# Moving TensorE's branch hint from the last down projection to the first combination

## The chip, the cores and the metric

The kernel runs on one core of a Trainium2 chip. The metric is the device time of one execution in microseconds (us), lower is better; several runs are taken and their median is given. A core has five engines with an instruction stream each: TensorE (PE, with PEld for its weight loads), VectorE (DVE), ScalarE (ACT), GpSimd (POOL) and SyncE (SP). Here SyncE issues all transfers of data.

## The reference

A gated linear attention feeds a soft mixture of experts. Per head (4 batches, 8 heads, 768 steps, 48 channels) a state is decayed by a gate and read by the query:

```
f = 1 / (1 + exp(-f_logit))
for t in range(768):
    state = f[:, :, t, :, None] * state + einsum('bhd,bhe->bhde', k[:, :, t], v[:, :, t])
    y[:, :, t] = einsum('bhd,bhde->bhe', q[:, :, t], state)
```

The outputs, laid side by side as x (3072 tokens, 384 channels), go through the mixture (8 experts, 4 slots each, 1024 hidden):

```
logits = x @ phi                                   # 3072 x 32
d = softmax of logits over the tokens;  slot_input = d.T @ x
slot_out[e] = maximum(slot_input[e] @ w1[e], 0) @ w2[e]
c = softmax of logits over the slots;   return c @ slot_out
```

## The kernel before

All arithmetic is in float32. The attention runs in 24 blocks of 128 tokens, in the chunked form (scores, masks, a state carried from block to block). It needs gates whose running products stay within a bound; the kernel computes beside the result a flag that says whether they do.

The mixture's tail follows the last block. `up` multiplies the 32 slot inputs with w1, `turn` transposes the hidden values, and then come three parts of 128 output channels each. For part p there are four down projections `dn{p}0` to `dn{p}3` (function `down`, matmuls at L822, 16 products of 128x128 in each), a copy (L830), one matmul that sums over the experts (L834), a copy into `s4` (L838), two combinations `cb{p}0` and `cb{p}1` (function `combine`, matmuls at L845), copies of the result into staging buffers (L854, L856, L859) and stores (L863), issued by SyncE.

The order on each engine is written down ahead of time by a planner, the class `Plan`: every operation is added with a cost, its dependences and a due time, `plan.schedule()` picks an order, and a loop over `plan.order` then emits the instructions in it. For TensorE the planner also counts instructions: a product costs `INS` = 4, a page holds `PAGE` = 256 of them, and a page is entered no sooner than `FETCH` = 5.8 us (a constant of the planner's costs) after the one before.

After the last operation each engine loads the flag into a register (`values_load`, L1038) and branches on it (`tc.If`, L1040). If the flag is set, a slow general computation, `general()`, follows. With the inputs here it isn't set, and every engine jumps over that code to a short closing part: at L1040 SyncE waits for the eight stores in flight, at L1095 all engines meet in a barrier.

Code for the general case is long, so the target of the jump lies far behind the branch. A branch hint is an instruction that each engine has ahead of its branch and that names the branch; its kind here is "LikelyTaken". The dictionary `hints` says ahead of which operation it stands: for SyncE, GpSimd, ScalarE and VectorE ahead of `si` (a copy, L757, at about 122 us), for TensorE ahead of `dn23`, the last down projection (it follows `dn22` in a run of 64 matmuls and loads that starts at 148.95 us). `cb00` is the first combination. On TensorE it starts at 142.19 us, behind the expert sum `so0` and one transposition, `ct5` (L704, 141.65 us). From there TensorE's order is `cb00`, `dn12`, `dn13`, `cb01`, `so1`, `dn20`, `dn21`, `cb11`, `dn22`, `dn23`, and after it `cb10`, `so2`, `cb20`, `cb21` and the branch.

Of the kernel before, what the change touches and what calls it, by code (L numbers as in the profile page):

```python
# [278 lines left out]
def gla_soft_moe_kernel(ctx: ExitStack, tc: tile.TileContext, q, k, f, v, fd, qd, kd, vd, phi, w1, w2, out):  # L279
# [13 lines left out]
    def P(shape, name, dt=F32):  # L293
        return pool.tile(shape, dt, tag=name, name=name)
# [60 lines left out]
    wb, wd, si = P([128, 1], "wb"), P([128, NS], "wd"), P([128, 3, NS], "si")  # L355
# [603 lines left out]


    EN = mybir.EngineType
    hints = {"si": [EN.SP, EN.Pool, EN.Activation, EN.DVE], "dn23": [EN.PE]}
    port = None
    for o in plan.order:
        if o["name"] in hints:
# [136 lines left out]
```

## Time and profile before

| | |
|---|---|
| median of 3 runs | 164.95 us (164.65 to 165.14) |
| the profiled execution: time, span | 164.98 us, 163.2 us |
| granted clock of TensorE, mean | 0.987 |
| busy: TensorE, VectorE, ScalarE, GpSimd | 147.3, 120.3, 99.0, 26.2 us |
| bytes moved | 54.01 MB in 17571 packets |
| q1 (data), q8 and q14 (instructions) | 17536, 21 and 14 packets |
| TensorE's hint, branch, next instruction | 149.2, 153.6, 156.2 us |
| end of the span | 163.2 us |

The span runs from the first instruction to the last; the time of an execution also has what lies around it. Times in the views are microseconds from the span's start. Letter q behind an engine's name marks its sequencer, which waits, branches and issues; these are not counted as the engine's busy time. A row of a line's view gives the operation, its count, the shortest, median and longest duration in nanoseconds, and the first and last start. The rows of the hints carry the line L1095, those of the branch L1040.

### The profile page before, as it was taken

To read this page: it belongs to the slowest core of one execution; us is meant where nothing else is said; L and a number is where in the kernel's file an instruction comes from. 1 tells how busy PE (TensorE), PEld (TensorE's weight loads), DVE (VectorE), ACT (ScalarE), POOL (GpSimd) and SP (SyncE) were. 2 spreads that over 40 slices of the span, in tenths; PEclk is the share of its full clock that TensorE was granted. 3 is DMA by queue.
4 is the path that set the end of the run, shared out by engine and by line. 5 is a ranking of instruction groups with operands and counts; after the bars stand their busy time and mean duration, and the time that the engine had idled before them with its cause. 6 is when DMAs were issued, how large, how long until landed. Compare 5 with 4: busy or idle time off the path is not lost.

```text
span 163.2 us, 5865 instructions
## 1 busy us (share of the span) xinstructions
PE 147.3 (90%) x2461; PEld 112.6 (69%) x2461; DVE 120.3 (74%) x234; ACT 99.0 (61%) x186; POOL 26.2 (16%) x43
## 2 busy tenths in 40 slices
PE   2998999999999999999999999999999999999600
PEld 2987777688877797878877887778753248777300
DVE  6789998899999999989999999999371113250410
ACT  4998977796959888783886967743440130033520
POOL 4001111050305020060306322160011000000000
PEclk9999999999999999999999999999999999999995
DMA  4999999999999799999999988618999998046891
GB/s 149 346 404 386 407 419 398 383 374 413 390 377 381 267 381 368 382 329 350 387 407 375 319 315 253 241 24 353 428 426 420 420 418 345 16 180 231 332 375 66
DMA packets 17571, 54.01 MB, mean 331 GB/s; under 512 B 1920, under 2 KB 5120, under 8 KB 14464
## 3 DMA queue, kind: packets, MB, share of 16 engines
q1 hardware_dynamic: 17536, 53.55, 87.0%
q8 instruction: 21, 0.34, 0.8%
q14 instruction: 14, 0.11, 0.2%
HBM read 48.82 MB, written 4.72 MB: 328 GB/s over the span
## 4 chain that ended last, share of the span: by engine, by line
PE 61%; DVE 14%; ACT 8%; DMA 7%; issue 3%; SPq 2%; POOL 1%; ACTq 0%; DVEq 0%; POOLq 0%
PE pr L541 12%; PE pr L581 6%; PE sg L612 6%; PE pr L572 5%; PE pr L788 5%; PE sg L822 5%; DVE as L544 4%; DMA ag<-in_f_dram 4%; PE sg L630 3%; PE sg L532 3%; PE pr L845 3%; DMA aq<-in_q_dram 3%; PE sg L659 2%; PE sg L553 2%; PE pr L822 2%
## 5 line engine op out<-in xcount | busy, mean ns | idle before, releaser
L544 DVE TENSOR_TENSOR as<-pr,tri 128x1024 f32<-128x1024 f32 x24 | 29.1, 1214 | 2.2 <-PE pr L541 1.5
L541 PE MATMUL pr<-aq,ak 48*128 48x128 f32 x384 | 27.9, 285 | 0.4 <-DVE as L544 0.2
L541 PEld LDWEIGHTS pr<-aq,ak 48*128 48x128 f32 x384 | 23.3, 187 | 5.0 <-issue 2.5
L581 PE MATMUL pr<-as,av 128*48 128x128 f32 x384 | 24.1, 274 | 1.2 <-DVE as L544 1.0
L581 PEld LDWEIGHTS pr<-as,av 128*48 128x48 f32 x384 | 20.2, 123 | 2.9 <-DVE as L544 2.1
L612 PE MATMUL sg<-ident,xT 128*128 128x128 f32 x96 | 15.2, 282 | 0.4 <-ACT ag L535 0.2
L527 POOL TENSOR_TENSOR aq<-aq,ac 128x512 f32<-128x512 f32 x9 | 11.4, 1281 | 25.0 <-ACT ac L502 8.7
L584 ACT COPY xT<-pr 128x512 f32<-128x512 f32 x20 | 11.5, 582 | 5.5 <-PE pr L581 5.4
L524 POOL TENSOR_TENSOR ak<-ak,af 128x512 f32<-128x512 f32 x6 | 7.7, 1279 | 35.3 <-ACT af L501 23.4
L572 PE MATMUL pr<-aq,st 48*48 48x128 f32 x320 | 13.1, 278 | 0.2 <-DVE aq L527 0.2
L502 ACT ACTIVATE ac<-ac 128x1024 f32<-128x1024 f32 (+1 forms) x13 | 12.9, 993 | 0.5
L612 PEld LDWEIGHTS sg<-ident,xT 128*128 128x128 f32 x96 | 10.4, 141 | 3.6 <-issue 1.5
L854 ACT COPY hm<-pr 128x768 f32<-128x768 f32 x7 | 5.5, 802 | 10.9 <-PE pr L845 10.9
L532 PE MATMUL sg<-ident,ak 128*128 128x128 f32 x80 | 11.9, 282 | 0.0
L487 DVE TENSOR_TENSOR_SCAN ac<-chain,af 128x256 f32<-128x256 f32 x16 | 10.9, 681 | 1.1 <-issue 1.1
L535 ACT COPY ag<-sg 128x512 f32<-128x512 f32 x17 | 9.4, 586 | 3.7 <-PE sg L532 3.7
L615 ACT COPY xr<-sg 128x384 f32<-128x384 f32 x17 | 8.1, 479 | 4.9 <-PE sg L612 4.8
L488 DVE TENSOR_TENSOR_SCAN ac<-chain,af 128x256 f32<-128x256 f32 x16 | 10.6, 665 | 0.0
L553 PEld LDWEIGHTS sg<-av,ag 128*48 128x48 f32 x320 | 8.6, 124 | 2.7 <-issue 1.2
L527 DVE TENSOR_TENSOR aq<-aq,ac 128x512 f32<-128x512 f32 x15 | 10.2, 685 | 0.3 <-POOL ak L524 0.2
L572 PEld LDWEIGHTS pr<-aq,st 48*48 48x48 f32 x320 | 8.0, 119 | 3.4 <-issue 2.0
L532 PEld LDWEIGHTS sg<-ident,ak 128*128 128x128 f32 x80 | 8.6, 141 | 2.2 <-issue 0.9
(142 smaller groups left out, 243.0 us busy)
## 6 DMA issues: line engine op xcount, KB each, us to landing
hm<-in_w_dram SPq DMA_DIRECT2D x17, 1024.0 KB, 8.0
ak<-in_k_dram SPq DMA_DIRECT2D x24, 256.0 KB, 5.9
aq<-in_q_dram SPq DMA_DIRECT2D x24, 256.0 KB, 5.8
av<-in_v_dram SPq DMA_DIRECT2D x24, 192.0 KB, 5.4
af<-in_f_dram SPq DMA_DIRECT2D x7, 512.0 KB, 5.6
out_dram<-hm SPq DMA_DIRECT2D x8, 384.0 KB, 3.8
ag<-in_f_dram SPq DMA_DIRECT2D x4, 512.0 KB, 5.9
out_dram<-hm SPq DMA_DIRECT2D x2, 768.0 KB, 4.3
```

What stands on the lines that cost most here:

```text
L487: nc.vector.tensor_tensor_scan(cx[:, : 2 * BT], chain, lx[:, : 2 * BT], 0.0, op0=ALU.mult, op1=ALU.add)
L502: add(f"p{n}", {"ACT": t_act(w)}, lambda e: nc.scalar.activation(flat(c_), flat(c_), AF.Exp, scale=-1.0), w=cs, prio=T(n, 1.2))
L527: tt(e)(flat(q_), flat(q_), flat(c_), op=ALU.mult)
L532: nc.tensor.transpose(pk[:, a], k_[:, a], ident)
L541: nc.tensor.matmul(ps[:, r, a], k_[rows[r], col(a)], queries(r, a), start=True, stop=True)
L544: tt(e)(sc_.rearrange("p r (m x) t -> p (r m) (x t)", x=2), bank(("sc", n)).rearrange("p r (m t) -> p (r m) t", m=2), tri.rearrange("p x t ...
L553: nc.tensor.matmul(pk[rows[r], col(a)], kp_[:, col(a), rows[r]], v_[:, 2 * a + r], start=True, stop=True)
L572: nc.tensor.matmul(py[at : at + D, r, a // 2], s0[rows[r], col(a)], queries(r, a), start=a < 2, stop=False, skip_group_check=True)
L581: nc.tensor.matmul(py[at : at + D, r, a // 2], v_[:, 2 * a + r], sc_[:, r, a], start=first and a < 2, stop=a >= 2, skip_group_check=True)
L584: copy(e)(xT[:, n % NXT].rearrange("p (r m) t -> p r (m t)", r=2), bank(("y", n))[:, :, : 2 * BT])
L612: nc.tensor.transpose(px[:, i], xT[:, n % NXT, i], ident)
L822: nc.tensor.matmul(po[32 * qq : 32 * qq + 32, :w], hT[:, j, 4 * kh + kk, 32 * qq : 32 * qq + 32], t[:, qq, kk], start=(j, kh, kk) == (0, 0 ...
```

## The change

TensorE's hint stands ahead of `cb00` instead of `dn23`. The other engines' hints and all operations stay where they are.

```
-    hints = {"si": [EN.SP, EN.Pool, EN.Activation, EN.DVE], "dn23": [EN.PE]}
+    hints = {"si": [EN.SP, EN.Pool, EN.Activation, EN.DVE], "cb00": [EN.PE]}
     port = None
     for o in plan.order:
         if o["name"] in hints:
             tc.mark_branch_hint_location("general", hint="LikelyTaken", engines=hints[o["name"]])
```

More of the change, by code (lines that the diff above doesn't have):

```diff
@@ L961, in gla_soft_moe_kernel @@
     EN = mybir.EngineType
-    hints = {"si": [EN.SP, EN.Pool, EN.Activation, EN.DVE], "dn23": [EN.PE]}
+    hints = {"si": [EN.SP, EN.Pool, EN.Activation, EN.DVE], "cb00": [EN.PE]}
     port = None
```

## The prediction

> **What bounds the kernel now.** I read the page first (busy shares, queues), then the chain of waits over the last 15 us, then the rows of the branch (L1040) and of its hints (recorded under L1095), and last the DMA queues in windows a tenth of a microsecond wide, because the hint can act only through an instruction fetch.
>
> The page: span, TensorE's busy time, the share of the chain, the two instruction queues.
>
> ```profile
> span 163.2 us, 5865 instructions
> PE 147.3 (90%) x2461; PEld 112.6 (69%) x2461; DVE 120.3 (74%) x234; ACT 99.0 (61%) x186; POOL 26.2 (16%) x43
> PE 61%; DVE 14%; ACT 8%; DMA 7%; issue 3%; SPq 2%; POOL 1%; ACTq 0%; DVEq 0%; POOLq 0%
> q8 instruction: 21, 0.34, 0.8%
> q14 instruction: 14, 0.11, 0.2%
> ```
>
> TensorE sets the time up to its last matmul. Queue q8 moved 0.34 MB in 21 packets, 16.2 KB each. TensorE ran 2 x 2461 = 4922 matmuls and weight loads; over 256 (the planner's PAGE) that is 19.2 pages, close to 21 packets. So I read q8 as TensorE's instruction stream, a page to a packet, and q14 as that of the other engines.
>
> The chain of waits over the end (start us, us, what), then the store and what SyncE does after the branch:
>
> ```profile
> 149.02 1.88 PE sg L822 x64
> 150.91 0.87 PE pr L845 x8
> ...
> 152.82 1.24 PE pr L845 x10
> ...
> 155.39 0.70 ACT hm L854
> ```
> ```profile
> L863 SPq DMA_DIRECT2D out_dram<-hm x10: 332/386/721, 144.2 to 156.4; - x10
> DMA to landing us min/median/max: 3.3/3.8/5.5
> ```
> ```profile
> L1040 SPq EVENT_SEMAPHORE  x8: 17/17/17, 161.1 to 161.9; - x8
> L1040 POOLq COMPARE_BRANCH  x1: 65/65/65, 123.4 to 123.4; - x1
> L1040 POOLq EVENT_SEMAPHORE  x1: 17/17/17, 128.7 to 128.7; - x1
> L1040 PEldq COMPARE_BRANCH  x1: 2482/2482/2482, 153.6 to 153.6; - x1
> L1040 ACTq COMPARE_BRANCH  x1: 68/68/68, 155.3 to 155.3; - x1
> L1040 DVEq COMPARE_BRANCH  x1: 84/84/84, 155.5 to 155.5; - x1
> L1040 PEldq EVENT_SEMAPHORE  x1: 51/51/51, 156.2 to 156.2; - x1
> L1040 ACTq EVENT_SEMAPHORE  x1: 17/17/17, 158.3 to 158.3; - x1
> L1040 SPq COMPARE_BRANCH  x1: 70/70/70, 158.9 to 158.9; - x1
> L1040 DVEq EVENT_SEMAPHORE  x1: 21/21/21, 159.3 to 159.3; - x1
> ```
> ```profile
> L1095 PEldq EVENT_SEMAPHORE  x2: 51/51/51, 162.7 to 163.2; - x2
> L1095 POOLq BRANCH_PREFETCH_HINT  x1: 43/43/43, 120.5 to 120.5; - x1
> ...
> L1095 DVEq BRANCH_PREFETCH_HINT  x1: 56/56/56, 122.5 to 122.5; - x1
> L1095 PEldq BRANCH_PREFETCH_HINT  x1: 45/45/45, 149.2 to 149.2; - x1
> ```
>
> The end is set thus: ScalarE's last copy ends at 155.39 + 0.70 = 156.1; SyncE issues the last store at 156.4; at the slowest landing, 5.5 us, it is down at 161.9, when the last of SyncE's eight semaphore waits at L1040 passes. The closing barrier ends at 163.2, and 1.78 us lie outside the span (164.98 - 163.2). TensorE's branch is the odd one: 2.48 us long, where the others record 65 to 84 ns. TensorE goes on at 156.2 and then waits for the closing barrier until 162.7: 6.5 us of slack behind the branch.
>
> **The change part by part.** The hint is one instruction of 45 ns on TensorE's sequencer. No wait, no issued transfer of data and no engine's order changes, and SP's and POOL's queues are not passed; the four other hints stay.
>
> First, the instruction itself. At the old place it is taken out of a stretch in which the matmul array is busy all the time, so nothing is gained there. At the new place it stands ahead of the first combination, where TensorE idles for VectorE's copy anyway:
>
> ```profile
> 141.65 0.27 PE L704 MATMUL sg<-ident,ltok 128*128 128x128 f32 x1
> 142.19 0.93 PE L845 MATMUL pr<-ltok,xT 32*128 32x384 f32 x8 [0.28 <-DVE xT L838]
> ```
> ```profile
> 142.00:146.00 4.00, 3.81 (x81) 2.52 (x82) 1.65 (x4) 0.90 (x2) 0.00 (x0) 1.00 0.25 95
> 146.00:150.00 4.00, 4.00 (x114) 3.13 (x117) 1.16 (x2) 1.61 (x3) 0.00 (x0) 1.00 0.79 302
> ```
> ```profile
> L834 PEldq EVENT_SEMAPHORE  x1: 51/51/51, 141.0 to 141.0; - x1
> ```
>
> The sequencer passes its last semaphore before that place at 141.0 (L834) and is held at the combination until VectorE's copy ends, shortly before 142.19. The 0.045 us lie inside that. Without this cover they cost 0.045 us, 0.03%. Taken: 0.
>
> Second, the fetch. In five answers of the DMA view, for 137.7 to 137.8, 143.3 to 143.4, 149.9 to 150.0, 153.4 to 153.5 and 158.1 to 158.3 us in this order, q8 has one packet each; the last line is 133 to 156 us, where it has these first four and no other:
>
> ```profile
> q8 instruction: 1, 0.02, 63.8%
> q8 instruction: 1, 0.02, 83.2%
> q8 instruction: 1, 0.02, 58.6%
> q8 instruction: 1, 0.02, 75.3%
> q8 instruction: 1, 0.02, 30.0%
> q8 instruction: 4, 0.07, 1.2%
> ```
>
> The share is that of 16 engines' time in the window, so the packets took 0.638 x 1.6 = 1.02, then 1.33, 0.94, 1.20 and (0.300 x 3.2) 0.96 us. The pages at 137.7, 143.3 and 149.9 come 5.6 and 6.6 us apart, at the pace of the stream. The one at 153.4 comes only 3.5 us later, starts before the branch (153.6) and is followed by TensorE's next instruction: it is down at 153.45 + 1.20 = 154.65, and TensorE goes on at 156.2, so 1.5 us pass from landing to use. I take it for the target's page, called by the hint 4.2 us earlier, and the branch's 2.48 us for the wait until it can be used. With the hint at about 141.1, 12.5 us ahead of the branch, the page should be there in time: the branch falls from 2.48 us to some 0.07 (like the others' 65 to 84 ns), and TensorE is through at 153.7. What hides this gain is SyncE's path, to which TensorE's 156.2 is not a party: the barrier waits for SyncE at 161.9. Taken: 0. If that cover were gone, the gain would be the 2.4 us.
>
> Third, the place of the fetch among the transfers. Now it takes 1.20 us on one of 16 DMA engines while the stores run, and the last stores land in up to 5.5 us where the fastest takes 3.3. Out of their way, the last landing can only come earlier, but SyncE itself does not reach its eight waits before 161.1, so the end moves by at most 161.9 - 161.1 = 0.8 us. At the other end, TensorE's next page (158.2 us now) simply moves to another place among the same stores: 0. I take 0, since all eight waits need time of their own after 161.1 and the fetch is one packet among a full queue's.
>
> Fourth, the fetch of the stream itself. At the new place the hint falls close to the page at 143.3. No row shows what two close calls on TensorE's fetch do to each other, so I bound it: 0, if they run side by side or the stream goes first, to a stall of the size of the two rivals below. I take 0: the hint's call stood behind a page of the stream in this trace too (149.9, 153.4), and TensorE was not held by it, with 4.00 of 4.00 us busy up to 150.
>
> Sum: 0 + 0 + 0 + 0 on 164.98 us of the profiled execution, which stands 0.03 us above the median of three runs, 164.95. Forecast: 164.95 us, no measurable change.
>
> [...]
>
> **The rivals.** *The hint does nothing there.* The target is dropped, or is fetched only when the stream reaches the branch's page. For it: GpSimd's hint at 120.5 stood 2.9 us ahead of its branch, VectorE's at 122.5 stood 33 us ahead, and both still waited 5.3 and 3.8 us behind the branch. Against it: TensorE's own fetch came ahead of its branch. At worst TensorE waits as GpSimd did, 5.3 us, and goes on at 153.6 + 5.3 = 158.9, still 3.8 us ahead of the barrier at 162.7. Time: 164.95.
>
> *The hint's page delays the page of the stream (slower).* If TensorE's fetches run one after another, the pair at 149.9 and 153.4 gives the pace, 3.5 us. A hint at 141.1 is served first, at about 143.3, and the stream's page follows at 146.8 rather than 143.3; it lands at about 147.8 and can be used at 149.3. It is needed 256 instructions after the page before: at (114 + 117) / 4.00 = 58 instructions per us in the window from 146 that is 4.4 us, and from the fetch at 143.3, called around 142.2, at 146.6 by the sequencer; its matmuls run up to 1 us later, at 147.6 to 147.9. TensorE would stand for about 149.3 - 147.9 = 1.4 us, and the chain is TensorE from there to 154.1 with hardly a gap. Time: 166.35; 0.5 us or less if the stream's page is called first or nearly so. It decides from the point where the hint is executed before the stream crosses into its next page, which the rows do not settle: 141.0 for the last semaphore before it, 143.3 for the page's packet.
>
> *The hint's page takes the place of the stream's next page (slower).* Then TensorE meets a missing page, whose price the rows of the branch show on other engines: 158.9 to 161.1 on SyncE is 2.2 us, on GpSimd 5.3. Time: 167.2 to 170.2. [...]
>
> *Faster.* The last stores land sooner without the fetch at 153.4 among them; at the 0.8 us bound that is 164.15; I price it at three quarters of the bound, 164.35. For it: landings between 3.3 and 5.5 us. Against it: one packet of 1.2 us on one engine, and SyncE's own 161.1.
>
> **How the numbers follow.** Three runs spread from 164.65 to 165.14; about 0.3%, 0.5 us, is what can be told from no change. Forecast with the page there in time 0.33; hint without effect 0.26; stream delayed 0.22, of which 0.02 within 0.3%; place taken 0.09; faster 0.10. So faster 0.10, same 0.61, slower 0.29. The likeliest time, 164.95, has 164.6 to 165.3 as its own range; the range for 8 in 10 runs from 164.3 (the larger part of the faster case) to 166.7 (the delayed stream and the spread of runs) and leaves out the taken place and part of the faster case.
>
> **What would show it.** Right: TensorE's branch below 0.1 us; its q8 packet for the target between 141 and 148 and none at 153; TensorE's last matmul still starting near 154.0; the last of SyncE's waits still at 161.9. Wrong: TensorE idle between 146 and 150, with "issue" as its releaser and no semaphore behind it (stream delayed or place taken); a branch still of 2.5 us, or a gap of 3 to 5 us behind it (no effect); the last landing before 161.4 (faster).

## The result, and the profile after

The changed kernel is slower. Beside the kernel before, with eight runs of each, its median was 165.85 us (165.26 to 166.22) against 164.96 us, a ratio of 1.0052 with a 95% interval of 1.0033 to 1.0071. Its profiled execution took 166.22 us, of which the span has 164.5.

TensorE's arithmetic is untouched. Three lines of the page after, then the windows by engine, then two pieces of the chain of waits (start us, us, what): from 146 to 150 us TensorE is busy for the same 4.00 us, and the last matmuls and ScalarE's last copy follow as before, 0.29 us later.

```profile
span 164.5 us, 5865 instructions
...
PE 147.7 (90%) x2461; PEld 112.9 (69%) x2461; DVE 120.2 (73%) x234; ACT 99.1 (60%) x186; POOL 26.2 (16%) x43
...
q8 instruction: 20, 0.33, 0.8%
```
```profile
146.00:150.00 4.00, 4.00 (x106) 3.05 (x106) 1.16 (x2) 1.41 (x2) 0.00 (x0) 1.00 0.80 308
```
```profile
153.11 1.24 PE pr L845 x10
...
155.68 0.70 ACT hm L854
```

The rows of the branch and of the hint, from the engines' sequencers (count, shortest, median and longest duration in ns, first and last start):

```profile
L1040 SPq EVENT_SEMAPHORE  x8: 17/17/17, 162.6 to 163.1; - x8
...
L1040 PEldq COMPARE_BRANCH  x1: 388/388/388, 153.9 to 153.9; - x1
L1040 PEldq EVENT_SEMAPHORE  x1: 51/51/51, 154.9 to 154.9; - x1
...
L1040 SPq COMPARE_BRANCH  x1: 70/70/70, 160.0 to 160.0; - x1
```
```profile
L1095 PEldq BRANCH_PREFETCH_HINT  x1: 45/45/45, 141.4 to 141.4; - x1
```

The hint does what it says. It stands at 141.4 us, TensorE's branch falls from 2.48 to 0.39 us, and TensorE is through at 154.9 instead of 156.2. Its stream of instructions does not hold it up, with 4.00 of 4.00 us busy from 146 to 150. But SyncE reaches its branch at 160.0 instead of 158.9 and its eight waits at 162.6 instead of 161.1. The reason stands one step earlier in SyncE's work, in the issues of the stores (L863; the second line is their landing):

```profile
L863 SPq DMA_DIRECT2D out_dram<-hm x10: 332/364/1677, 144.5 to 157.9; - x10
DMA to landing us min/median/max: 2.3/3.7/4.9
```

The longest issue takes 1677 ns where it was 721, and the last starts at 157.9 instead of 156.4. In order of time (start us, us), SyncE in two overlapping windows after, and in two before:

```profile
155.71 2.10 SPq L863 DMA_DIRECT2D out_dram<-hm  x2
...
156.13 2.52 SPq L863 DMA_DIRECT2D out_dram<-hm  x2
```
```profile
155.84 0.41 SPq L863 DMA_DIRECT2D out_dram<-hm  x1
...
156.36 0.72 SPq L863 DMA_DIRECT2D out_dram<-hm  x1
```

The two rows of after say that the issue at 155.71 and the next one end together at 157.81, and that the next one starts at 156.13: it is the one of 1.68 us, against 0.41 us before. Queue q8 in the window 156.05 to 156.15 us of the changed kernel:

```profile
q8 instruction: 1, 0.02, 82.8%
```

A page of TensorE's instructions starts in that tenth of a microsecond and takes 0.828 x 1.6 = 1.32 us. It is the page that TensorE calls once it has jumped: it starts 1.2 us behind TensorE's next instruction (154.9), where it came at 158.2 before, 2.0 us behind (156.2), and where the branch is held it moves along with it (e13, e14 and e1 below). Reading on the trace's own clock, it starts at 156.10, 0.03 us ahead of the issue, and is down at 157.43; the issue ends 0.38 us after that.

About 0.3 us of this execution's 1.3 us more of span have another cause: TensorE's matmuls at L788 stand at 128.80 instead of 128.51 us, 12 us ahead of any difference between the kernels. From execution to execution the start of ScalarE's last copy moves between 154.8 and 155.7 us whatever the hint. So below I also give the stretch from the start of ScalarE's last copy (155.27 before, 155.57 after) to the end of the span: 7.97 us before, 8.92 after.

### The profile page after: what moved, and what is told of

Its sections match the earlier page's. It is cut to its first block, busy times and chain, and to the rows that moved or that the text cites. A ratio compares the mean times of both kernels' runs of the same rounds, so it can differ in the third digit from the quotient of the medians.

```text
span 164.5 us, 5865 instructions
## 1 busy us (share of the span) xinstructions
PE 147.7 (90%) x2461; PEld 112.9 (69%) x2461; DVE 120.2 (73%) x234; ACT 99.1 (60%) x186; POOL 26.2 (16%) x43
## 4 chain that ended last, share of the span: by engine, by line
PE 58%; DVE 12%; DMA 11%; ACT 8%; SPq 3%; issue 2%; ACTq 0%; DVEq 0%
PE pr L541 10%; DMA av<-in_v_dram 6%; PE pr L581 6%; PE sg L612 5%; PE pr L788 5%; PE pr L572 5%; DMA aq<-in_q_dram 5%; PE sg L822 4%; DVE as L544 4%; PE sg L630 3%; SPq L456 3%; PE pr L845 3%; PE sg L659 2%; PE sg L532 2%; PE sg L553 2%; PE pr L822 2%
```

## The experiments

My theory after the comparison: *a page of TensorE's instructions that meets a store issue of SyncE holds that issue until the page is down, and the early hint moves the page after the branch onto the fifth of the last six issues.* The rivals: *the early hint costs by itself*, through its fetch among the stores or in the stream, and *drift*, that is, nothing but the spread between executions.

The table sums up all profiles; the runs are told below it. "Page" is the start of TensorE's pages on q8 from 4 us ahead of ScalarE's last copy on, counted from that copy's start; SyncE's last four issues start at -0.56, 0.14, 0.56 and 1.1 in each of them where none is held. "Held to" gives the start of TensorE's branch. "Issue" is the longest of these four, "stretch" runs from that copy's start to the end of the span; all in us.

| run | hint, TensorE's branch | page | issue | stretch | ratio (95% interval) |
|---|---|---|---|---|---|
| before | last down | -1.83, 2.92 | 0.72 | 7.97 | |
| e6, before again | last down | -1.77, 2.85 | 0.93 | 8.22 | |
| e16, before again | last down | -1.25, 3.50 | 0.72 | 7.99 | |
| after | first combination | 0.53 | 1.68 | 8.92 | 1.0052 (1.0033 to 1.0071) |
| e5, after again | first combination | 0.65 | 1.49 | 8.47 | 1.0016 (0.9996 to 1.0036) |
| e9, after again | first combination | 0.66 | 1.48 | 8.40 | 1.0001 (0.9972 to 1.0030) |
| e15, after again | first combination | 0.68 | 1.69 | 8.46 | 1.0052 (1.0031 to 1.0072) |
| e13 | first combination, held to 155.4 | 2.90 | 0.72 | 7.94 | 0.9988 (0.9973 to 1.0002) |
| e14 | first combination, held to 156.5 | 3.90 | 0.72 | 8.10 | 1.0005 (0.9984 to 1.0027) |
| e1 | first combination, held to 157.2 | 4.62 | 0.71 | 8.41 | 0.9990 (0.9965 to 1.0015) |
| e10, e1 again | first combination, held to 157.8 | 4.73 | 0.72 | 8.14 | 0.9997 (0.9976 to 1.0019) |
| e2 | last down, held to 156.9 | -0.15, 4.88 | 1.02 | 9.19 | 1.0022 (1.0000 to 1.0044) |
| e3 | none | 0.62, 5.16 | 1.49 | 8.82 | 1.0010 (0.9983 to 1.0037) |
| e4 | behind the last down | -3.28, 0.31 | 1.75 | 8.71 | 1.0002 (0.9972 to 1.0031) |

**TensorE's branch held, with the early hint (e1) and the late one (e2).** One matmul more on TensorE, ahead of the flag's load; it overwrites a bank that ScalarE's last copy reads, and so waits for the end of that copy (it reads the staging buffer of an earlier copy, not the last as the expectation has it).

```
+    nc.tensor.matmul(pairs[1][:, 0, :128], stage[2][1][:, :128], ones, start=True, stop=True)
     bad = nc.values_load(gbad[:1, :1], min_val=0, max_val=1)
```

> The changed kernel (hint ahead of the first combination), with one more matmul on TensorE ahead of its branch, which reads the staging buffer that ScalarE fills last, so that TensorE reaches its branch at about 156.5 us instead of 153.9; its result isn't used. Collision theory: the page that TensorE calls after its branch then comes at about 158.3, behind SyncE's last store issue, no issue of SyncE's takes over 0.75 us, and the time is that of the kernel before, ratio 0.998 to 1.002. Rival (the early hint itself costs, by its fetches among the first stores or in TensorE's stream): the time stays 0.5% above, ratio 1.004 to 1.007.

> Control: the kernel before with the same extra matmul. The target's page comes at 153.4 as before, TensorE goes on at about 156.8 instead of 156.2 and calls the following page at about 158.5 instead of 158.2. Collision theory: ratio 0.998 to 1.002. If the extra matmul itself costs or gains something, this shows how much; the rival (the early hint itself costs) expects this one 0.5% faster than its twin with the early hint.

With the early hint and the branch held, the time can't be told from that of the kernel before, 0.9990. The stores' issues and SyncE's branch are back where they were:

```profile
L863 SPq DMA_DIRECT2D out_dram<-hm x10: 332/386/737, 144.0 to 156.2; - x10
```
```profile
L1041 PEldq COMPARE_BRANCH  x1: 388/388/388, 157.2 to 157.2; - x1
...
L1041 SPq COMPARE_BRANCH  x1: 70/70/70, 158.8 to 158.8; - x1
```

So with TensorE jumping later the early hint shows no cost; that speaks against the first rival. The control, e2, missed its expectation: the target's page came at 155.27 instead of 153.4, fell on the issue at 0.14 and held it for 1.02 us. Read afterwards this is what the theory asks for, and e2, which the first rival wanted 0.5% faster than e1, is if anything slower (1.0022 against 0.9990, with intervals that overlap).

**No hint (e3), and the hint one operation later (e4).** The one has TensorE's entry taken out of `hints`, the other `"cb10": [EN.PE]`.

> The kernel before without TensorE's hint. TensorE's branch at 153.7 then finds no target: its page is fetched at 155 to 156 and the following page two or three us later. Collision theory: the target's fetch itself now falls on SyncE's store issues at 155.4 to 156.4, one of them takes 1 us or more, ratio 1.003 to 1.008. Rival (the early hint itself costs): nothing early is fetched, TensorE has slack up to 162.7, ratio 0.998 to 1.002.

> The kernel before with TensorE's hint one operation later, behind the last down projection instead of ahead of it (about 0.9 us later). Collision theory: the target's page comes later by up to 0.9 us, at 153.4 to 154.5, TensorE goes on by up to 0.9 us later, at 156.2 to 157.1, and the following page comes at 158.2 to 159, so nothing meets SyncE's issues from 154.7 to 157.1: ratio 0.998 to 1.002. Rival (the early hint itself costs, the later the better): ratio 0.996 to 1.000.

Without a hint TensorE's branch takes 4.56 us, and no page comes between 151 and 155.4; the first one at 155.46 is the target's. It holds an issue for 1.49 us:

```profile
L863 SPq DMA_DIRECT2D out_dram<-hm x10: 332/364/1492, 143.8 to 157.0; - x10
```
```profile
L1040 PEldq COMPARE_BRANCH  x1: 4557/4557/4557, 153.3 to 153.3; - x1
...
L1040 PEldq EVENT_SEMAPHORE  x1: 51/51/51, 157.9 to 157.9; - x1
```

In e4 the expectation was wrong on the moment: the target's page came earlier than before, at 151.7, not later, so TensorE went on at 154.6 and its next page hit the issue at 0.56 (1.75 us). Both profiles have the long issue and the long stretch that the theory asks for; their times, 1.0010 and 1.0002, don't tell them from the kernel before, with intervals of 0.3% to each side and a loss of 0.4% to be seen. For e3 the theory had asked for 1.003 to 1.008, which it missed. In time these two are inconclusive.

**The changed kernel and the kernel before again (e5, e6).**

> The changed kernel once more, beside its held twin of the first call and the kernel before. Collision theory: TensorE's page after the branch comes at 155.5 to 156.5 us again, one of SyncE's last four store issues takes over 1 us, and the ratio to the kernel before is 1.003 to 1.007, 0.4% or more above the held one's 0.999. Rival (the 0.5% came from drift between executions, since TensorE's matmuls were 0.29 us late already before the hint): ratio 0.998 to 1.002.

> The kernel before once more, for a second look at its profile. Collision theory: where the target's page is fetched by 153.5 us, no store issue from 154.5 us on takes over 0.75 us; where it slips to 155 us or later, as in the held twin with the late hint (155.3), one issue takes 1 us or more and the span is 163.8 to 164.6. Rival (drift alone): issues and span have nothing to do with each other.

The held issue is there again (1.49 us) and the stretch is 8.47 us, but the ratio, 1.0016, is less than at first, short of the expected 1.003 to 1.007 and inside the range of drift. The second profile of the kernel before has 8.22 us; its last issue takes 0.93 us, with no page of TensorE's between -0.3 and 2.8.

**SyncE's hint later (e7), and with the branch held (e8).** SyncE's entry moves from `si` to `"st02": [EN.SP]`; e8 has also the early hint and the matmul of e1.

> The kernel before with SyncE's hint ahead of the second store (about 145 us) instead of at 121.6 us. SyncE's branch at 158.9 is followed by its next instruction only 2.2 us later. If a late hint is fetched as TensorE's was, an instruction page comes for SyncE between 146 and 150, SyncE reaches its eight waits at about 159, and the end is set by the last landing at 161.9: ratio 0.997 to 1.000. If the hint does nothing on SyncE wherever it stands, the gap stays 2.2 us and the ratio is 0.999 to 1.001.

> The held kernel with the early hint and SyncE's hint ahead of the second store: no page of TensorE's at 153 to 157, and SyncE's target fetched early if late hints work there. Collision theory: no issue over 0.75 us, and with SyncE's gap gone the end is the last landing, about 161.3: ratio 0.993 to 0.997. If SyncE's hint does nothing: as the held kernel, ratio 0.997 to 1.001.

The hint on SyncE does nothing there. It stands at 144.2 us in e7, no page comes on q14 from 145 to 156 us, and SyncE still waits behind its branch, from 158.5 to 160.8:

```profile
L1040 SPq EVENT_SEMAPHORE  x8: 17/17/17, 160.8 to 161.3; - x8
...
L1040 SPq COMPARE_BRANCH  x1: 70/70/70, 158.5 to 158.5; - x1
```

The times are those of a hint that does nothing, 1.0013 (0.9991 to 1.0034) and 0.9999 (0.9973 to 1.0025). For the collision both count as free cases: TensorE's pages at -1.54 and 2.57 in e7 and 4.59 in e8, stretches of 7.93 and 8.03 us.

**The pair on one chip (e9, e10), and the last store issued by ScalarE (e11, e12).** In the last two `store` takes `nc.scalar` for the store of the last copy; e11 is otherwise e1, e12 the kernel before.

> The changed kernel, timed on the same chip and in the same rounds as its held twin (next run). Collision theory: TensorE's page at 155.5 to 156.5 us, SyncE's second to last store issue over 1 us, the stretch from the start of ScalarE's last copy to the end of the span 8.4 to 9.0 us, ratio to the kernel before 1.001 to 1.006. Rival (nothing but drift): that stretch 7.9 to 8.3 us as in the kernel before.

> The held twin (early hint, TensorE's branch behind ScalarE's last copy) once more. Collision theory: no page of TensorE's between 151 and 158 us, no store issue over 0.75 us, the stretch from ScalarE's last copy to the end 7.9 to 8.5 us, ratio 0.997 to 1.001, and 0.2% or more below the changed kernel of this call. Rival (drift alone): as the changed kernel.

> The held twin, with the last store issued by ScalarE behind its last copy instead of by SyncE. SyncE issues three of the last four stores and reaches its branch about 1 us earlier, so that its target's page is there before the last landing. If SyncE's own path (branch, 2.2 us, eight waits) sets the end: the stretch from ScalarE's last copy to the end is 7.4 to 7.9 us and the ratio 0.994 to 0.999. If the last landing sets it: unchanged, ratio 0.997 to 1.001.

> The kernel before (late hint, no hold), with the last store issued by ScalarE. Same theories as for the run before it: 7.4 to 7.9 us and ratio 0.995 to 1.000 if SyncE's own path sets the end, unchanged if the last landing does.

Issues and stretches of the pair are as expected (1.48 us and 8.40; 0.72 and 8.14), but the ratios, 1.0001 and 0.9997, don't separate the two; 0.2% or more between them was expected. ScalarE's store was a miss: 1.0027 (1.0004 to 1.0050) in e11, 1.0001 (0.9974 to 1.0027) in e12, stretches of 8.91 and 8.28 us. SyncE does branch 1.3 us earlier in e11, but its next instruction comes no earlier:

```profile
L1041 SPq EVENT_SEMAPHORE  x8: 17/17/17, 162.0 to 162.6; - x8
...
L1041 SPq COMPARE_BRANCH  x1: 70/70/70, 157.5 to 157.5; - x1
```

4.5 us pass from branch to next instruction, where it was 2.8 in e1 and 2.2 in the kernel before. What holds the page of SyncE's target I did not separate; as far as the packets of q14 can be told apart, in all these profiles it starts 4.2 us or more behind the start of ScalarE's last copy, while the stores are still on their way.

**The moment of the page alone (e13, e14).** The early hint is left, and only the copy that TensorE's branch waits for is changed: the third-last (e13) or the second-last (e14).

```
+    nc.tensor.matmul(pairs[2][:, 0, :128], stage[2][1][:, :128], ones, start=True, stop=True)   # e13
+    nc.tensor.matmul(pairs[0][:, 0, :128], stage[2][2][:, :128], ones, start=True, stop=True)   # e14
```

> The changed kernel (early hint) with TensorE's branch held behind ScalarE's third-last copy (ends 0.6 us before the last one starts) by a matmul that overwrites the bank this copy reads. TensorE's page after the branch then comes 1.2 to 2.2 us after the start of ScalarE's last copy, not at 0.5 to 0.7. Collision theory: the issue at 0.56 stays under 0.6 us, but the last issue, at 1.1, meets the page if it comes by about 1.6 and then takes 1 us or more; stretch from the last copy to the end 8.4 to 9.0 us in that case, 7.9 to 8.4 if the page comes later than 1.8. Rival (the early hint costs by itself): 8.4 to 9.0 with short issues.

> The same, with TensorE's branch held behind ScalarE's second-last copy (ends about 0.1 us after the last one starts). The page comes 2.0 to 3.2 us after the start of the last copy, behind the end of the last issue at 1.8. Collision theory: no issue over 0.75 us (the last one up to 0.95 as in the kernel before), stretch to the end 7.9 to 8.4 us, ratio 0.997 to 1.001, below the changed kernel's. Rival (the early hint costs by itself): 8.4 to 9.0 us, ratio as the changed kernel's.

> The changed kernel. Collision theory: the issue at 0.56 over 1 us, stretch 8.4 to 9.0 us, none of its runs in the lowest quarter of the kernel before's, ratio 1.000 to 1.005. Rival (drift alone): ratio 0.998 to 1.002 and its lowest runs as low as those of the kernel before.

> The kernel before. Collision theory: page of the target about 1.8 us ahead of ScalarE's last copy, the one after it 2.2 to 3 us behind its start, no issue over 1 us, stretch 7.9 to 8.3 us. Rival (drift alone): the stretch varies as much as the changed kernel's, up to 8.9 us.

In the same rounds the changed kernel is at 1.0052 (1.0031 to 1.0072) and its two held twins at 0.9988 and 1.0005: their intervals don't touch that of the changed kernel. In e13 TensorE's branch stands at 155.4 instead of 153.7 in e15, its page at 2.9 instead of 0.68 (the first row is q8 from 158.0 to 158.1 us), and the issue is free:

```profile
q8 instruction: 1, 0.02, 58.1%
```
```profile
L863 SPq DMA_DIRECT2D out_dram<-hm x10: 332/386/730, 144.0 to 156.2; - x10
```
```profile
L1041 SPq EVENT_SEMAPHORE  x8: 17/17/17, 160.9 to 161.7; - x8
...
L1041 ACTq COMPARE_BRANCH  x1: 68/68/68, 155.1 to 155.1; - x1
...
L1041 PEldq COMPARE_BRANCH  x1: 398/398/398, 155.4 to 155.4; - x1
```

and in e15 it is held (the first row is q8 from 156.05 to 156.15 us):

```profile
q8 instruction: 1, 0.02, 62.5%
```
```profile
L863 SPq DMA_DIRECT2D out_dram<-hm x10: 332/364/1687, 144.3 to 157.8; - x10
```
```profile
L1040 SPq EVENT_SEMAPHORE  x8: 17/17/17, 161.9 to 162.5; - x8
```

The pages came later than I had reckoned (2.9 in e13, not 1.2 to 2.2; 3.9 in e14, not 2.0 to 3.2), so what happens when one meets the last issue was not tried. The third profile of the kernel before, e16, has no issue over 0.75 us and a stretch of 7.99 us, as the theory expected.

**Taken together.** The stretch is 8.40 to 9.19 us in the seven profiles with a page of TensorE's between -0.2 and 0.7 (mean 8.71: after, e5, e9, e15, e2, e3, e4) and 7.93 to 8.41 us in the nine with none there (mean 8.08: before, e6, e16, e1, e10, e13, e14, e7, e8; e11 and e12 issue otherwise and are left out). The gap is 0.63 us, 0.4%. For the changed kernel against the kernel before alone it is 8.56 (four profiles) less 8.06 (three), 0.50 us, 0.3%. The two groups just meet, at e1's 8.41 and e9's 8.40. Two nearer steps of the chain separate them clearly. The held issue ends 0.38 to 0.57 us after the page is down in all seven, though the pages take from 0.92 to 1.62 us; and SyncE's branch, counted from the start of ScalarE's last copy, stands at 4.08 to 4.49 us in the seven and at 3.63 to 3.87 in the nine. It is behind this branch that the profiles differ by up to 1 us for other reasons: SyncE's next instruction comes 2.1 to 2.8 us after it in the nine, 2.2 to 3.2 in the seven.

In time, all 42 runs of the changed kernel lie at 165.20 us or above, and so do the 12 of e2, while 47 of the 99 runs of the kernel before that were timed beside the changed kernel lie below that, and 25 of the 48 of its held twins (e1, e10, e13, e14). Against the theory, 8 of the 24 runs of e3 and e4 lie below it too, although their profiles show a held issue. A profile shows one execution; in how many executions of these two an issue was held, no run shows.

## Why the prediction was wrong, point by point

The forecast was no measurable change, 164.95 us; measured were 165.85 us, slower by 0.52% with an interval of 0.33 to 0.71%. That this lies inside the range of 164.3 to 166.7 us is luck: the range was that wide for a delayed stream. The case "slower" had 0.29, and neither of the two mechanisms that stood for it took place.

The step that failed is the third term, the place of the fetch among the transfers. It looked at the target's page, which leaves the stores, and dismissed the other page in half a sentence: TensorE's next page "simply moves to another place among the same stores: 0". Its new place follows from rows that stood in the prediction. TensorE went on at 156.2 and called the page of 158.2, so 2.0 us later; with TensorE through at 153.7, as forecast, that gives about 155.7, in the middle of the issues that run from 154.7 to 157.1; measured were 154.9 and 156.1. And what an issue does under a page of TensorE's was in the trace of before too. SyncE's loads at L456, with their longest issue, and three of them in order of time:

```profile
L456 SPq DMA_DIRECT2D ak<-in_k_dram x24: 327/328/1220, 1.7 to 96.8; - x24
```
```profile
54.90 1.20 SPq L456 DMA_DIRECT2D ag<-in_f_dram  x1
...
88.40 0.33 SPq L456 DMA_DIRECT2D aq<-in_q_dram  x1
88.78 1.22 SPq L456 DMA_DIRECT2D ak<-in_k_dram  x1
```

In the windows 54.7 to 54.8 and 88.4 to 88.5 us, just ahead of the two long ones, q8 has one packet each:

```profile
q8 instruction: 1, 0.02, 63.8%
q8 instruction: 1, 0.02, 72.1%
```

These two take 1.2 us, where most of the loads' issues take 0.33. There the loads have time to spare: no engine waits for a landing from 54.9 to 65 us, nor from 88.7 to 100. The last stores have none: SyncE's load of the flag, ahead of its branch, starts at 157.1 us, where the last issue ends (156.36 + 0.72). So the term is 1.1 to 1.3 us on one issue (1.48 to 1.69 in place of 0.41). Of this 0.6 us reach SyncE's branch (4.32 us behind the start of ScalarE's last copy in the mean of four profiles, 3.72 in three of before) and 0.5 us the end: SyncE's load of the flag was shorter behind the late issue (0.64 us, where it was 1.09 before), and the path behind the branch varies.

A page on its way does not hold every issue. The one at 88.40 has the page start 0.08 us after it and still takes 0.33 us; the next one is held. In e5 a page starts at 150.89 and takes 0.94 us, and the store issue at 150.95 takes 0.35. In all 18 profiles 342 of SyncE's issues have a page of TensorE's that starts before 0.33 us of the issue are over and stays on its way for 0.15 us of it or more. Read off afterwards, what separates them is SyncE's issue before: where that one started at most 0.6 us ahead of the page, or while the page was on its way, 145 of 158 issues took over 0.5 us; elsewhere 3 of 184 did. In the four profiles of the changed kernel the issue before the held one started 0.39 to 0.55 us ahead of the page. So the place of a page has to be compared with a pair of issues, not with one. Why this is so no run shows, and pages are not the only thing that lengthens an issue: 105 of the 256 issues over 0.5 us met none of TensorE's.

The other terms held. The hint itself costs nothing and is covered: the idle time ahead of the first combination is 0.28 us with it as without. That the hint called the target's page in the kernel before is confirmed by e3, where that page is missing and the branch takes 4.56 us. TensorE's earlier end brings nothing, since the end hangs on SyncE. The branch fell to 0.39 us, not 0.07. The stream was not held: in the changed kernel q8 has one packet from 144.6 to 156 us, one less than before in all, so the target's page did not come on top of the stream's pages. That disposes of both rivals that stood for "slower", and "the hint does nothing" is refuted by the branch. The rival "faster" has half a case: e13, with the target early and the page after it out of the way, was the fastest version tried, 0.9988 with an interval of 0.9973 to 1.0002, which doesn't tell it from the kernel before.

That a page called so far ahead is still at hand at the branch was my assumption in the second term; no row of before shows it. In the changed kernel it held: the target's page was called at the latest by 148.4 us, where q8 has its last packet before 156, and was at hand at 153.9, where the branch took 0.39 us (4.56 in e3), with TensorE's own stream running without a stall (4.00 of 4.00 us busy from 146 to 150). How many pages TensorE holds at once no run shows: if the packet at 148.37 us is the target's page, only 189 recorded instructions of TensorE start between it and the branch, fewer than the planner's 256 to a page.

What stays open is the size in time. Four timings of the same change gave 1.0052, 1.0016, 1.0001 and 1.0052, two of them clear of 1 and two not; the held issue is in all four profiles, with a stretch that is longer by 0.3% of the time than in three profiles of before, and a spread of some 0.9 us in the start of ScalarE's last copy lies over it.

## What to carry to other kernels

Here an instruction fetch was a transfer among the others, 16 KB on q8 that took 0.92 to 1.62 us in the seven profiles with a held issue, and TensorE, through 1.3 us earlier, called its next page 2.1 us earlier (156.1 instead of 158.2). So when a branch or a hint moves, work out where every later page falls, and look whether another engine issues transfers there, one close behind the other, on the path that sets the end. What was saved on the engine with slack was lost on the one without: SyncE reached its branch 1.1 us later (160.0 instead of 158.9). And the price of such a meeting stood in the trace already, as the longest duration of a group whose median is short (1220 against 328 ns at L456).

## What the runs showed of the hardware that was not expected

- A store issue of SyncE's held by a page of TensorE's (16 KB on q8) took 1.0 to 1.75 us instead of 0.33 to 0.41, and ended 0.38 to 0.57 us after the page was down. Over all 18 profiles the issues that were held are nearly always those whose predecessor on SyncE had started from 0.6 us ahead of the page on (145 of 158 held, 3 of 184 elsewhere).
- A hint well ahead of the branch did not add a page on TensorE: 20 packets on q8 with the early hint, 21 with the late one and 21 with none. With the early hint the page that starts 4.7 to 7.2 us ahead of ScalarE's last copy, where the others have one of the stream's, may be the target's itself; no run separates the two.
- The same hint on SyncE at 121.6 or 144.2 us called no page that can be told: q14 has the same two packets between 120 and 156 us with either (127.0 and 132.0 us, 126.6 and 131.9). SyncE, ScalarE and VectorE waited 2.1 to 4.8 us behind their branches in every profile. Why the hint worked on TensorE alone in these runs was not found.
